# A gap of four words in the transposed tokens of the feed-forward: the first product reads a two-dimensional pattern

## The chip, the cores and the metric

The kernel runs on one core of a Trainium2 chip. The metric is the device time of one execution in microseconds; a profile of one execution gives its span, from the first to the last instruction.

## What is computed

Inputs are q, k, v of shape (8, 8, 576, 64) and two weights of a feed-forward, 512 x 2048 and 2048 x 512. Cut to what matters:

```python
out_d  = sm_attn(mean4(q), mean4(k), mean4(v))        # attention on tokens pooled by 4
out_up = repeat(out_d, 4)
scores = where(abs(i - j) < 4, q @ k.T / 8, -1e9)      # local attention
x = heads_to_channels(out_up + softmax(scores) @ v)    # (8, 576, 512)
mixed = real(fft(fft(x, axis=1), axis=2))
u  = x + mixed
un = (u - mean(u)) / sqrt(var(u) + 1e-6)               # over the 512 channels
result = u + maximum(un @ w_ch1, 0) @ w_ch2
```

## The kernel before

The 8 x 576 = 4608 tokens make 36 tiles of 128. The first third of the execution is attention and the mixing of tokens and channels. Then comes the feed-forward, which the change touches. It goes over nine blocks (class `Block`) of four tiles, 512 tokens, and in each block over f = 0 to 15, the sixteen slices of 128 hidden channels.

Before a block, each of its four tiles is normalised (`un`), transposed on TensorE in four pieces of 128 x 128 (`turn`, L733), and split into a high part (`turn_high`, ScalarE, L739, rounds to float32r) and the remainder (`turn_low`, VectorE, L742). Both parts are written into `unT`, of which there are two: `unT0` for the blocks 0, 2, 4, 6, 8 and `unT1` for the blocks 1, 3, 5, 7. In each partition `unT` holds, for the part x and the channel slice c, the 512 tokens of the block in a row; `turned` gives the place of one tile of 128 in it.

For each f, `first` (L762) makes twelve matmuls into one PSUM bank `hps`: for the four channel slices c, `w1h` with the high part, `w1l` with the high part, `w1h` with the low part. The weight slice of 128 x 128 is stationary, and the 512 tokens in `unT[:, x, c, :]` move. ScalarE takes the relu into `hh` (L766), VectorE the remainder into `hl` (L770), and `second` makes twelve matmuls (L780 to L782) into four accumulators `acc`, one for each tile, with `hh` or `hl` stationary and `w2h` or `w2l`, 512 words in a row, moving. So a block has 16 x 12 first and 16 x 12 second products. At its end VectorE adds `acc` to the tokens (L786), and they are stored.

The weights' high and low parts stay in SBUF for the whole feed-forward. Those of f = 0 and 1 lie in the pool `res`, those of f = 2 to 4 in the pool `pt`, 5 to 8 in `middle`, the others in `more`. `unT0` lies in the pool `early`, `unT1` in `middle`; these pools are opened at `close_b`, `close_a`, `close_e` and `close_d`, when the tiles of the earlier stages at their places are no longer used.

The order of all work is written out by hand: `at(t, fn)` puts each step into a list with a nominal time, and the steps are issued to their engines in the order of those times. In `Block.plan`, the second product of f comes after the first product of f + 1, and the transposes of the next block's tiles are put between the groups of the current block.

Two other places matter to the reading of the profile. In the channel mix, the last matmul of a group (L609) has the moving operand `signs.unsqueeze(1).to_broadcast([P, HD, 2])`: 256 times the same two words. The mask of the local attention (L388) moves 64 words of bfloat16 eight times over.

Of the kernel before, what the change touches and what calls it, by code (L numbers as in the profile page):

```python
# [9 lines left out]
F32R = mybir.dt.float32r  # L10
# [47 lines left out]
TILES = 4  # L58
# [7 lines left out]
def kernel(  # L66
# [14 lines left out]
    nc = tc.nc  # L81
    P = 128
# [4 lines left out]
    NCC = DM // P  # L87
# [23 lines left out]
    def weight_tiles(pool, fs, which=(1, 2)):  # L111

        for f in fs:
            for w in which:
                shape = [P, NCC, P] if w == 1 else [P, DM]
                wts[f, w] = [pool.tile(shape, F32R, name=f"w{w}{part}{f}", bufs=1) for part in "hl"]
# [11 lines left out]
    unTs = {}  # L128
# [85 lines left out]
    pools = {}  # L214

    def bank(name, rows=P):
        banks.append(banks.pop(0))
        return banks[-1].tile([P, DM], F32, name=name, tag="ps")[:rows]
# [135 lines left out]
    class Unit:  # L354
# [123 lines left out]
        def plan(self):  # L478
            t = 4 * self.u
            for fn, (first, step) in ((self.load, AT["qk"]), (self.sum_in, AT["sums"])):  # L480
                at(pooled_at(self.b) + first + step * self.m, fn)
            at(t + AT["load_v"][0], self.load_v)
            stages = [self.scores, self.maxima, self.exps, self.transpose_p, self.copy_p, self.values, self.result]
            for d, fn in zip(AT["local_steps"], stages):
                at(t + d, fn)
# [22 lines left out]
    class Mix:  # L508
# [130 lines left out]
        def plan(self):  # L639
            t = mix_at(self.b)  # L640

            local = list(reversed(range(NSL)))
            first, step, first_m, step_m = AT["halves"]
            for i, slot in enumerate(local):
                at(t + first + step * i, self.half_sum, slot)
                at(t + first_m + step_m * i, self.half_difference, slot)
            for begin, name, these in (
                (pooled_end(self.b), "pooled_splits", (NSL, NSL + 1)),
                (t, "splits", local),
            ):  # L650
                first, step, odd, high, low = AT[name]
                for i, slot in enumerate(these):
                    u = begin + first + step * i
                    at(u, self.channels_even, slot)
                    at(u + odd, self.channels_odd, slot)
                    at(u + high, self.split_high, slot)
                    at(u + low, self.split_low, slot)
# [25 lines left out]
    def pool(name, bufs=1, **kw):  # L683
        return ctx.enter_context(tc.tile_pool(name=name, bufs=bufs, reuse_waits="tile", **kw))
# [3 lines left out]
    class Block:  # L688
# [44 lines left out]
                nc.tensor.transpose(tp[:, c * P : (c + 1) * P], self.un[i][:, c * P : (c + 1) * P], ident)  # L733

        def turned(self, i, x):
            return unTs[self.n % 2][:, x, :, i * P : (i + 1) * P]

        def turn_high(self, i):
            nc.scalar.copy(out=self.turned(i, 0), in_=self.tp[i].rearrange("p (c n) -> p c n", c=NCC))  # L739
# [15 lines left out]
        def first(self, f):  # L755

            unT = unTs[self.n % 2]
            w1h, w1l = wts[f, 1]
            hps = self.hps[f] = bank("hps")[:, : TILES * P]
            mms = [(a, x, c) for a, x in ((w1h, 0), (w1l, 0), (w1h, 1)) for c in range(NCC)]  # L760
            for i, (a, x, c) in enumerate(mms):
                nc.tensor.matmul(hps, a[:, c, :], unT[:, x, c, :], start=(i == 0), stop=(i == len(mms) - 1))  # L762

        def high(self, f):
            hh = self.hh[f] = pools["pt"].tile([P, TILES * P], F32R, name="hh", bufs=2)
# [65 lines left out]
    def close_b():  # L831
        p1.close()
        pools["early"] = pool("early")
        unTs[0] = pools["early"].tile([P, 2, NCC, TILES * P], F32R, name="unT0")

    def close_a():
        plocal.close()
# [8 lines left out]
    def close_e():  # L846
        pseq.close()
        middle = pool("middle")
        unTs[1] = middle.tile([P, 2, NCC, TILES * P], F32R, name="unT1")
        weight_tiles(middle, range(*CHUNKS[1:3]))  # L850

    def close_d():
        pmix.close()
        weight_tiles(pool("more"), range(*CHUNKS[2:]))

    at(t_b, close_b)
    at(t_a, close_a)
    at(t_e, close_e)
    at(t_d, close_d)
    for i in range(TILES):  # L860
# [9 lines left out]
    t = t_a + AT["ffn"][0]  # L870
    starts = {}
    for n, f0, f1 in [(0, 0, ROUND), (1, 0, ROUND), (0, ROUND, NF)] + [(n, ROUND * (n == 1), NF) for n in range(1, NBLK)]:
        starts[n] = t
        t = blocks[n].plan(t, f0, f1)
# [15 lines left out]
    t = 0.0  # L890
    for n, x in enumerate(quarters):
        if x.f < CHUNKS[0]:
            decode(n, first + step * n, ahead)
        else:
            begin = [t_a + ahead_later, t_e, t_d][sum(x.f >= c for c in CHUNKS[1:3])]
            t = max(t + step_later, begin + 0.3)
# [139 lines left out]
```

## Time and profile before

| | |
|---|---|
| time, median of 3 runs | 1229.01 us |
| lowest and highest run | 1224.79 and 1229.82 us |
| span of the profiled execution | 1224.5 us (the page gives no time for it beside the span) |
| mean granted TensorE clock | 0.979 |
| PE busy | 1175.8 us, 8336 matmuls |
| first product, L762 | 1728 matmuls of 128 x 128 by 128 x 512 |
| second product, L780 to L782 | 1728 matmuls of the same shape |
| a whole block of the feed-forward | 89.46 to 89.50 us |

How to read it: PE is TensorE's matmul row, PEld its weight loads, which run beside matmuls. The recorded duration of a matmul reaches into the next one, so the price of a matmul in a dense stretch is the distance from its start to the next start. In a timeline a row may stand for several instructions (x4) that follow one another; the first number is the start of the first of them in microseconds from the span's start.

### The profile page before, as it was taken

Reading aid. Unit: us, or ns where it says so; the run is one execution under the profiler, and the core shown is the slowest. Engines: PE = TensorE matmul, PEld = TensorE weight load, DVE = VectorE, ACT = ScalarE, POOL = GpSimd, SP = SyncE. Lnnn points to the kernel's source line nnn. Section 1 sums busy time; section 2 is a strip of 40 time slices with the busy share of each in tenths; the row PEclk is TensorE's granted clock in tenths of the full one; section 3 lists DMA queues with packets and bytes.
Section 4 is the critical chain, followed back from the end, with each engine's and each line's share of the span. In section 5 each row is a group of like instructions: output and inputs, shape, how many; then the busy total and the mean of one; then the engine's idle time right before and its main releaser. Section 6 shows DMA issues by size and latency. Waiting matters only on the chain.

```text
span 1224.5 us, 20569 instructions
## 1 busy us (share of the span) xinstructions
PE 1175.8 (96%) x8336; PEld 977.2 (80%) x8336; DVE 596.9 (49%) x1218; ACT 356.1 (29%) x1038; POOL 321.0 (26%) x397
## 2 busy tenths in 40 slices
PE   5799999999997799999999999999999999999998
PEld 4687887888885677888888888888888888888887
DVE  3778887998969789834122222222221222221212
ACT  2655556655553334411011111011111111111110
POOL 2326356447528466620100100100100100100000
PEclk7899999999998899999999999999999999999999
DMA  9855565667624444440400400400400400300000
GB/s 289 224 169 163 171 180 163 189 196 207 167 69 138 118 134 120 130 112 1 103 2 1 103 1 1 104 1 1 104 1 1 103 1 1 103 1 1 35 1 35
DMA packets 50462, 111.45 MB, mean 91 GB/s; under 512 B 6120, under 2 KB 6248, under 8 KB 50040
## 3 DMA queue, kind: packets, MB, share of 16 engines
q1 hardware_dynamic: 42000, 88.66, 22.5%
q0 software_dynamic: 8368, 21.48, 9.6%
q8 instruction: 66, 1.08, 0.4%
q14 instruction: 28, 0.23, 0.1%
HBM read 81.82 MB, written 28.34 MB: 90 GB/s over the span
## 4 chain that ended last, share of the span: by engine, by line
PE 77%; DVE 11%; DMA 5%; issue 3%; POOL 2%; ACT 1%; SPq 0%; DVEq 0%; POOLq 0%; ACTq 0%
PE hps L762 31%; PE acc L780 10%; PE acc L782 10%; PE acc L781 10%; PE y L571 4%; PE mix L609 3%; PE av L454 2%; DMA vsum<-in_vg_dram 2%; PE avd L309 1%; DMA raw<-in_wq_dram 1%; PE sc L395 1%; DMA ud<-odt 1%; DVE sums L381 1%; PE tpn L733 1%; DVE wt L174 1%
## 5 line engine op out<-in xcount | busy, mean ns | idle before, releaser
L770 DVE SCALAR_TENSOR_TENSOR hl<-hps,hh 128x512 fp32r<-128x512 f32 x144 | 99.3, 690 | 460.1 <-ACT hh L766 460.1
L762 PE MATMUL hps<-unT,w1h 128*128 128x512 f32 x1152 | 311.5, 392 | 0.0
L762 PEld LDWEIGHTS hps<-unT,w1h 128*128 128x128 f32 x1152 | 216.3, 189 | 45.9 <-DVE unT L742 0.3
L766 ACT ACTIVATE hh<-hps 128x512 fp32r<-128x512 f32 x144 | 86.1, 598 | 515.8 <-PE hps L762 515.8
L780 PE MATMUL acc<-w2h,hh 128*128 128x512 f32 x576 | 227.5, 395 | 1.7 <-DVE ut L786 1.6
L782 PE MATMUL acc<-w2h,hl 128*128 128x512 f32 x576 | 225.6, 392 | 0.2 <-DVE hl L770 0.2
L781 PE MATMUL acc<-w2l,hh 128*128 128x512 f32 x576 | 225.0, 391 | 0.0
L762 PE MATMUL hps<-unT,w1l 128*128 128x512 f32 x576 | 155.7, 392 | 0.0
L780 PEld LDWEIGHTS acc<-w2h,hh 128*128 128x128 f32 x576 | 108.3, 188 | 25.6 <-DVE ut L786 1.5
L782 PEld LDWEIGHTS acc<-w2h,hl 128*128 128x128 f32 x576 | 108.3, 188 | 24.7 <-DVE hl L770 1.3
L762 PEld LDWEIGHTS hps<-unT,w1l 128*128 128x128 f32 x576 | 108.8, 189 | 23.6
L781 PEld LDWEIGHTS acc<-w2l,hh 128*128 128x128 f32 x576 | 108.3, 188 | 22.1
L718 POOL TENSOR_TENSOR rstd<-rstd,mhalf 128x1 f32<-128x1 f32 x36 | 20.5, 571 | 340.4 <-DVE rstd L717 340.4
L705 POOL DMA_DIRECT2D ut<-ud x40 | 36.2, 1154 | 207.8 <-DMA ut<-um 207.7
L413 ACT ACTIVATE sb<-sc,mx 128x64 f32<-128x64 f32 x320 | 69.8, 329 | 1.3
L609 PE MATMUL mix<-chanm,yh 128*128 128x512 f32 (+1 forms) x192 | 65.8, 425 | 3.1 <-DVE xs L613 2.0
L549 POOL TENSOR_TENSOR fl<-xeo,fh 128x512 fp32r<-128x512 f32 (+1 forms) x40 | 55.1, 1383 | 43.5 <-ACT fh L544 43.5
L454 PE MATMUL av<-vaug,pT 64*64 64x65 f32 x1280 | 48.4, 225 | 6.9 <-POOL pT L442 4.9
L454 PEld LDWEIGHTS av<-vaug,pT 64*64 64x64 f32 x1280 | 42.5, 138 | 15.6 <-POOL pT L442 5.1
L522 POOL TENSOR_TENSOR xm<-xa,xb 128x512 f32<-128x512 f32 x24 | 32.9, 1372 | 81.5 <-DVE xb L472 70.6
L742 DVE TENSOR_TENSOR unT<-tpn,unT 128x512 fp32r<-128x512 f32 x36 | 24.7, 687 | 55.2 <-ACT unT L739 55.2
L395 PEld LDWEIGHTS sc<-qkT 64*64 64x64 f32 x1280 | 46.5, 141 | 3.5 <-issue 0.8
(102 smaller groups left out, 1552.6 us busy)
## 6 DMA issues: line engine op xcount, KB each, us to landing
qkT<-in_qk_dram SPq DMA_DIRECT2D x40, 512.0 KB
raw<-in_wq_dram SPq DMA_DIRECT2D x64, 256.0 KB
vaug<-in_vw_dram SPq DMA_DIRECT2D x40, 260.0 KB
ud<-odt SPq DMA_DIRECT2D x16, 576.0 KB
out_dram<-ut SPq DMA_DIRECT2D x36, 256.0 KB
ut<-um SPq DMA_DIRECT2D x32, 256.0 KB
ut<-ud POOLq DMA_DIRECT2D x32, 256.0 KB, 5.4
vsum<-in_vg_dram POOLq DMA_DIRECT2D x24, 292.5 KB, 4.8
```

Source lines behind the costliest of these rows:

```text
L395: nc.tensor.matmul(sc[r, a * W : (a + 1) * W], self.qkT[r, 0, a // 2, o : o + W], self.qkT[r, 1, a // 2, o : o + W], start=False, stop=Tru ...
L413: nc.scalar.activation(out=self.sb[:, a], in_=self.sc[:, a * W : (a + 1) * W], func=AF.Exp, scale=0.125, bias=self.mx[:, a : a + 1],)
L454: nc.tensor.matmul(av[r, a, :], pT[r, 4 * hh + a], va[r, 4 * hh + a, :], start=True, stop=True)
L549: nc.gpsimd.tensor_sub(out=l, in0=self.x[t], in1=h.bitcast(F32))
L571: nc.tensor.matmul(y, l, r, start=(i == 0), stop=(i == len(mms) - 1))
L609: nc.tensor.matmul(to, l, r, start=(i == 0), stop=(i == len(mms) - 1))
L762: nc.tensor.matmul(hps, a[:, c, :], unT[:, x, c, :], start=(i == 0), stop=(i == len(mms) - 1))
L766: nc.scalar.activation(out=hh, in_=self.hps[f], func=AF.Relu)
L770: nc.vector.scalar_tensor_tensor(out=hl, in0=self.hps[f], scalar=0.0, in1=self.hh[f].bitcast(F32), op0=ALU.max, op1=ALU.subtract)
L780: nc.tensor.matmul(acc, hh, w2h, start=start, stop=False)
L781: nc.tensor.matmul(acc, hh, w2l, start=False, stop=False)
L782: nc.tensor.matmul(acc, hl, w2h, start=False, stop=stop)
```

## The change

Both `unT` get a gap of four words (16 bytes) after each run of tokens: `unT0` has four runs of 128 tokens, 132 words apart, `unT1` has two runs of 256 tokens, 260 words apart. `turned` finds a tile's place in the new layout, and `first` reads the runs as a pattern of two dimensions and names its output in PSUM, which lies as before, by the same two dimensions. `unT0` takes 512 bytes more in each partition, `unT1` 256.

```diff
         def turned(self, i, x):
-            return unTs[self.n % 2][:, x, :, i * P : (i + 1) * P]
+            u = unTs[self.n % 2]
+            n = TILES // u.shape[3]
+            return u[:, x, :, i // n, i % n * P : i % n * P + P]
...
             hps = self.hps[f] = bank("hps")[:, : TILES * P]
+            n = unT.shape[3]
             mms = [(a, x, c) for a, x in ((w1h, 0), (w1l, 0), (w1h, 1)) for c in range(NCC)]
             for i, (a, x, c) in enumerate(mms):
-                nc.tensor.matmul(hps, a[:, c, :], unT[:, x, c, :], start=(i == 0), stop=(i == len(mms) - 1))
+                nc.tensor.matmul(
+                    hps.rearrange("p (n t) -> p n t", n=n),
+                    a[:, c, :],
+                    unT[:, x, c, :, : TILES * P // n],
+                    start=(i == 0),
+                    stop=(i == len(mms) - 1),
+                )
...
-        unTs[0] = pools["early"].tile([P, 2, NCC, TILES * P], F32R, name="unT0")
+        unTs[0] = pools["early"].tile([P, 2, NCC, TILES, P + 4], F32R, name="unT0")
...
-        unTs[1] = middle.tile([P, 2, NCC, TILES * P], F32R, name="unT1")
+        unTs[1] = middle.tile([P, 2, NCC, 2, TILES // 2 * P + 4], F32R, name="unT1")
```

## The prediction

> **What bounds the kernel now.** I read the head of the page first: the engines' busy time, the span in 40 slices and the chain that ended last.
>
> ```profile
> span 1224.5 us, 20569 instructions
> PE 1175.8 (96%) x8336; PEld 977.2 (80%) x8336; DVE 596.9 (49%) x1218; ACT 356.1 (29%) x1038; POOL 321.0 (26%) x397
> PE   5799999999997799999999999999999999999998
> PEclk7899999999998899999999999999999999999999
> PE 77%; DVE 11%; DMA 5%; issue 3%; POOL 2%; ACT 1%; SPq 0%; DVEq 0%; POOLq 0%; ACTq 0%
> PE hps L762 31%; PE acc L780 10%; PE acc L782 10%; PE acc L781 10%; PE y L571 4%; PE mix L609 3%; PE av L454 2%; DMA vsum<-in_vg_dram 2%; PE avd L309 1%; DMA raw<-in_wq_dram 1%; PE sc L395 1%; DMA ud<-odt 1%; DVE sums L381 1%; PE tpn L733 1
> ```
>
> TensorE is busy 96% of the span, the granted clock is full in the last two thirds, and the chain runs 77% through PE. The first product of the feed-forward (L762), the line that the change edits, is 31% of the chain. So what one of its 1728 matmuls gains or loses is seen in the end. The windows on whole blocks of four token tiles confirm it:
>
> ```profile
> 593.46:682.92 89.46, 89.46 (x401) 73.70 (x400) 21.79 (x40) 11.62 (x20) 6.61 (x9) 1.00 0.14 36
> 1040.80:1130.30 89.50, 89.50 (x402) 73.74 (x401) 21.79 (x40) 11.62 (x20) 5.73 (x8) 1.00 0.14 36
> ```
>
> The columns are length, then busy time of PE, PEld, DVE, ACT and POOL, the granted clock, the DMA share and GB/s. PE has no gap in a block; DVE (21.8 of 89.5) and ACT (11.6) have much room.
>
> The recorded duration of a matmul (390 ns) overlaps with the next, so its price is the distance from one start to the next. The timeline gives it: a settled group in the middle of a block, the start of a block, and a group after the transposes of the next block's tokens.
>
> ```profile
> 638.41 1.07 PE L762 MATMUL hps<-unT,w1h 128*128 128x512 f32 x4
> 639.32 1.07 PE L762 MATMUL hps<-unT,w1l 128*128 128x512 f32 x4
> 640.23 1.07 PE L762 MATMUL hps<-unT,w1h 128*128 128x512 f32 x4
> 641.13 0.39 PE L780 MATMUL acc<-w2h,hh 128*128 128x512 f32 x1
> ...
> 643.86 0.39 PE L762 MATMUL hps<-unT,w1h 128*128 128x512 f32 x1
> ```
>
> ```profile
> 593.46 1.10 PE L762 MATMUL hps<-unT,w1h 128*128 128x512 f32 x4
> 594.39 1.09 PE L762 MATMUL hps<-unT,w1l 128*128 128x512 f32 x4
> 595.33 1.10 PE L762 MATMUL hps<-unT,w1h 128*128 128x512 f32 x4
> 596.26 0.40 PE L780 MATMUL acc<-w2h,hh 128*128 128x512 f32 x1
> ```
>
> ```profile
> 618.39 0.60 PE L733 MATMUL tpn<-ident,un 128*128 128x128 f32 x4
> 618.74 0.48 PE L780 MATMUL acc<-w2h,hh 128*128 128x512 f32 x1
> 619.05 0.40 PE L781 MATMUL acc<-w2l,hh 128*128 128x512 f32 x1
> ...
> 621.60 0.39 PE L762 MATMUL hps<-unT,w1h 128*128 128x512 f32 x1
> ```
>
> Settled, twelve first products take 641.13 - 638.41 = 2.72 us, 227 ns each, and twelve second products 643.86 - 641.13 = 2.73 us, the same. At the block's start, where the weights are those of f = 0, in a pool of their own, twelve take 596.26 - 593.46 = 2.80 us, 233 ns each. After the transposes eleven take 621.60 - 619.05 = 2.55 us, 232 ns each, and then the pace settles. So the pace of the same instruction depends on where its operands lie and on what ran just before; it is not a fixed price.
>
> **What a two-dimensional read costs here.** The trace has two matmuls of 512 columns whose moving operand is a two-dimensional pattern: the signs in the channel mix (256 runs of two words, f32r) and the mask (8 runs of 64, bf16). Their rows in the views by tile, with those of the first product:
>
> ```profile
> L609 PE MATMUL mix<-signs,yz x24: 377/378/380, 90.1 to 436.2; 128*128 128x512 f32 x16, 128*64 128x512 f32 x8
> L388 PE MATMUL sc<-maskb,identb x80: 375/376/632, 15.6 to 354.9; 64*64 64x512 bf16 x80
> L762 PE MATMUL hps<-unT,w1h x1152: 387/390/775, 389.6 to 1214.8; 128*128 128x512 f32 x192
> L762 PE MATMUL hps<-unT,w1l x576: 386/390/629, 390.5 to 1213.9; 128*128 128x512 f32 x192
> L739 ACT CAST unT<-tpn x36: 578/587/589, 378.8 to 1111.4; 128x512 fp32r<-128x512 f32 x36
> L742 DVE TENSOR_TENSOR unT<-tpn,unT x36: 675/691/693, 381.4 to 1112.0; 128x512 fp32r<-128x512 f32 x36
> ```
>
> The slowest of the 24 sign matmuls (380) is shorter than the fastest of 1728 first products (386); the medians differ by 12 ns. The starts say the same in a place where a sign matmul stands between one-dimensional ones of the same shape:
>
> ```profile
> 426.74 0.40 PE L609 MATMUL mix<-chanm,yh 128*128 128x512 f32 x1
> 426.98 0.40 PE L609 MATMUL mix<-chanm,yl 128*128 128x512 f32 x1
> 427.21 0.38 PE L609 MATMUL mix<-signs,yz 128*128 128x512 f32 x1
> 427.42 0.40 PE L780 MATMUL acc<-w2h,hh 128*128 128x512 f32 x1
> 427.66 0.40 PE L781 MATMUL acc<-w2l,hh 128*128 128x512 f32 x1
> ```
>
> Distances: 0.24, 0.23, then 0.21 for the sign matmul, then 0.24 again. So wrapping from run to run costs nothing there, 256 times over, and the contiguous read of 512 words is the slower one. What the rows do not separate: both two-dimensional patterns read few words again and again (step 0), while the changed unT reads 512 different ones. That is the point on which the forecast stands or falls.
>
> [...]
>
> **The change, part by part.**
> - The first product, 1728 matmuls (9 blocks x 16 f x 12): same count, same weights, same 512 columns. unT0 (blocks 0, 2, 4, 6, 8) is read as 4 runs of 128, unT1 (the four odd blocks) as 2 runs of 256. Ends of the price: 12 ns less (the sign row) and 6 ns more (233 against 227, the pace at which the same read goes in its unsettled form). I take the sign row, as the nearest with this kind of pattern, for both tiles: 1728 x 12 = 20.7 us less, all on the path, since PE has no gap.
> - The second product (L780 to L782) is not edited, but it follows a group with another pace, and the rows after the transposes show that a disturbed pace needs about eleven matmuls to settle: 11 x (232 - 227) = 55 ns for a group. If it happens in each of the 144 groups: 8 us back; if in none: 0. I take 25 ns for a group, under half, because the transposes are a harsher break than a change of pace: 3.6 us back.
> - The writers of unT (L739 on ACT, L742 on DVE, 36 each): they already write four runs of 128, at steps of 512 words; the step becomes 528 or 520. Instruction count and elements stay. I cost it at nothing: both engines are mostly idle in a block, and their 587 and 691 ns lie beside PE's second products. If that cover were gone, 36 x 0.1 us, for a tenth of a microsecond more each, would be 4 us.
> - The output view of hps: still 512 contiguous words; nothing.
> - Memory: unT0 grows by 512 bytes in each partition, unT1 by 256, so tiles above them move up by as much. That may change which freed tile a new one waits for between 370 and 590 us, where pools change over. No row prices it: 0 taken, 3 us either way kept for the range.
> - No wait, DMA or queue entry is added, and none moved past another.
>
> Sum: -20.7 + 3.6 = -17.1 us. The profiled execution has a span of 1224.5 us, so its span would become 1207.4. The median of the three runs, 1229.0, is 4.5 above that span; taking the same difference off the median gives 1212.
>
> **Rivals.**
> 1. No change: 1229. The sign and mask matmuls are fast because they read the same few words again, not because they are two-dimensional, and a run of 128 different words is read at the pace of 512. For it: the mask is bf16, the signs are two words. Against it: the pace of the contiguous read does vary with placement, so it isn't at a limit of bandwidth. [...]
> 2. Slower by a lost lock. The settled pace needs the moving read and the weight load beside it to fall into step; the gap shifts every run by four words against the weights, the step is lost, and every first product goes at 233. Place: groups now settled, about 144 less the 18 of f = 0 and 1 in nine blocks; price 0.08 us each (2.80 - 2.72), 126 x 0.08 = 10 us, 1239; with the second product disturbed after each, 126 x 0.055 = 7 us more, 1246. It shows as slower once more than half of those groups (6 of 10 us) are unsettled. For it: the f = 0 groups, where only the weights' place differs. Against it: the settled pace comes back by itself after each break.
> 3. Slower by a restart. The 12 ns that a contiguous read has over the sign matmul is a price for beginning a read, and each run pays it: unT0 3 x 12 x 960 matmuls = 35 us, unT1 1 x 12 x 768 = 9 us, 1273. Against it: 256 runs of the sign matmul pay nothing. It decides from 2 ns a run on (about 7 us).
>
> **How the numbers follow.** A measurement of this kernel tells some 0.5% (6 us) from no change: its three runs lie 5 us apart. Forecast: 0.46, own range 1204 (no second product disturbed: 1208; the 18 groups of f = 0 and 1 lose their 0.08 us too: 1 us; the memory's 3 us fall on the good side) to 1222 (every second product disturbed, 1216, and a third of the 12 ns not won, 7 us). No change 0.26. Lost lock 0.19, restart 0.09. So faster 0.46, same 0.26, slower 0.28. The range 1204 to 1242 leaves out the restart and the worst of the lost lock above, and a little below: some 2 in 10.
>
> **What would show it.** Right: the median duration of L762 in the view by tile near 378, twelve first products in about 2.58 us, blocks of 89.5 us near 87.5, even and odd blocks alike. Rival 1: 390 and 89.5 as before. Rival 2: L762 at 396 with groups of 2.80 us, blocks above 90. Rival 3: even blocks some 7 us longer, odd ones 2. Even and odd blocks that differ would say that the length of a run counts. Wrong in its second step: L780 to L782 with starts of 0.23 to 0.24 throughout after faster first products. The forecast fails if the sign matmul's pace comes from its few words.

## The result, and the profile after

The change made the kernel slower: 1233.51 us (median of 10 runs, 1229.19 to 1236.84) against 1226.05 (1221.06 to 1230.08), ratio 1.006 with a 95% interval of 1.004 to 1.0079. That is 0.6%: small, but clear of the noise. The profiled execution took 1230.93 us, with a span of 1229.2. The head of its page and the line of the chain:

```profile
span 1229.2 us, 20578 instructions
PE 1179.9 (96%) x8336; PEld 974.2 (79%) x8336; DVE 597.2 (49%) x1218; ACT 356.4 (29%) x1038; POOL 318.5 (26%) x397
...
PE hps L765 31%; PE acc L789 10%; PE acc L790 10%; PE acc L791 10%; PE y L571 4%; PE mix L609 4%; PE av L454 2%; DMA vsum<-in_vg_dram 2%; PE sc L395 2%; PE avd L309 2%; DMA raw<-in_wq_dram 1%; DMA ud<-odt 1%; DVE sums L381 1%; PE tpn L733 1
```

The same 8336 matmuls keep PE busy 4.1 us longer. The busy times of the others moved by 3 us at most (PEld 977.2 to 974.2, POOL 321.0 to 318.5, DVE and ACT 0.3 each), and none of them bounds a block. The windows on one even block (unT0, four runs) and one odd block (unT1, two runs) show where:

```profile
592.13:682.18 90.05, 90.05 (x401) 73.67 (x400) 21.79 (x40) 11.62 (x20) 6.62 (x9) 1.00 0.14 36
682.18:772.77 90.59, 90.59 (x402) 73.62 (x400) 21.77 (x40) 11.63 (x20) 5.73 (x8) 1.00 0.14 35
```

Both were 89.47 before. If all nine blocks lose as much, five even blocks by 0.58 and four odd ones by 1.12 make 7.4 us, about the difference of the medians (7.5). In the two profiled executions themselves the stretch from the third block to the end grew by 6.0 us, from 631.0 (1224.5 - 593.46) to 637.1 (1229.2 - 592.13); the stretch before it came out 1.3 us shorter, so the spans differ by 4.7 only. PE still has no gap: the matmuls follow one another more slowly. The view by tile has it in the durations of the first product (medians 390 before), and the timeline in its starts, for an even and an odd block:

```profile
L765 PE MATMUL hps<-unT,w1h x1152: 388/393/774, 386.7 to 1219.4; 128*128 128x512 f32 x192
L765 PE MATMUL hps<-unT,w1l x576: 388/393/618, 387.6 to 1218.5; 128*128 128x512 f32 x192
```

```profile
648.66 1.08 PE L765 MATMUL hps<-unT,w1h 128*128 128x512 f32 x4
...
651.43 0.39 PE L789 MATMUL acc<-w2h,hh 128*128 128x512 f32 x1
...
654.17 0.40 PE L765 MATMUL hps<-unT,w1h 128*128 128x512 f32 x1
...
710.49 1.09 PE L765 MATMUL hps<-unT,w1h 128*128 128x512 f32 x4
...
713.28 0.39 PE L789 MATMUL acc<-w2h,hh 128*128 128x512 f32 x1
...
716.02 0.39 PE L765 MATMUL hps<-unT,w1h 128*128 128x512 f32 x1
```

Twelve first products take 2.77 us in the even block and 2.79 in the odd one (2.72 when settled before), and the twelve second products after them 2.74 (2.73). Start by start, the twelve of the even block repeat with the four channel slices: 234, 230, 225, 234 ns, then twice 231, 230, 225, 234. The slices lie 64 bytes further on each, modulo 256, so the pace seems to go with the place of what is read. The groups no longer settle at 227 ns, and the two dimensions bring nothing: no matmul is near the sign matmul's 378 ns.

### The profile page after: what moved, and what is told of

The parts are those of the page before. It is cut to its first block, busy times and chain, and to the rows that moved or that the text cites. A ratio compares the mean times of both kernels' runs of the same rounds, so it can differ in the third digit from the quotient of the medians.

```text
span 1229.2 us, 20578 instructions
## 1 busy us (share of the span) xinstructions
PE 1179.9 (96%) x8336; PEld 974.2 (79%) x8336; DVE 597.2 (49%) x1218; ACT 356.4 (29%) x1038; POOL 318.5 (26%) x397
## 4 chain that ended last, share of the span: by engine, by line
PE 79%; DVE 11%; DMA 5%; issue 2%; POOL 2%; ACT 1%; SPq 1%; DVEq 0%; POOLq 0%; ACTq 0%
PE hps L765 31%; PE acc L789 10%; PE acc L790 10%; PE acc L791 10%; PE y L571 4%; PE mix L609 4%; PE av L454 2%; DMA vsum<-in_vg_dram 2%; PE sc L395 2%; PE avd L309 2%; DMA raw<-in_wq_dram 1%; DMA ud<-odt 1%; DVE sums L381 1%; PE tpn L733 1%; PE sp L264 1%
## 5 line engine op out<-in xcount | busy, mean ns | idle before, releaser
L549 POOL TENSOR_TENSOR fl<-xeo,fh 128x512 fp32r<-128x512 f32 (+1 forms) x40 | 52.5, 1318 | 46.8 <-ACT fh L544 46.8
L741 ACT CAST unT<-tpn 128x512 fp32r<-128x512 f32 x36 | 21.1, 586 | 97.6 <-PE tpn L733 97.6
```

Source lines behind the costliest of these rows:

```text
L549: nc.gpsimd.tensor_sub(out=l, in0=self.x[t], in1=h.bitcast(F32))
```

## The experiments

Each kernel was profiled in one execution. What is compared is the length of blocks, from the starts of three successive blocks in the timeline (an even block, then an odd one); this length repeats within 0.05 us inside one execution. Of the kernels in this section only the last was timed more than once. Numbers of bytes below that the kernels' shapes and paddings don't give are places of tiles in the compiled programs, which no trace holds.

**Runs without a gap.** Does a pattern of several dimensions cost or bring anything?

```diff
         def turned(self, i, x):
+            i = (0, 2, 1, 3)[i]
             return unTs[self.n % 2][:, x, :, i * P : (i + 1) * P]
...
-                nc.tensor.matmul(hps, a[:, c, :], unT[:, x, c, :], start=(i == 0), stop=(i == len(mms) - 1))
+                m = unT[:, x, c, :].rearrange("p (h t n) -> p t h n", h=2, t=2)
+                to = hps.rearrange("p (t h n) -> p t h n", h=2, t=2)
+                nc.tensor.matmul(to, a[:, c, :], m, start=(i == 0), stop=(i == len(mms) - 1))
```

> Before with the first product reading four runs of 128 words without any gap: tiles 1 and 2 of a block change places in unT, and the runs are read in the order 0, 2, 1, 3, so that the pattern cannot be merged into one of 512 words. All runs start where they did, at the same place within 64 bytes as the weights. Theory P (place: what counts is how the moving words lie against the weights within some 64 bytes, the number of runs is free): blocks of four tiles stay at 89.47 us, twelve settled first products take 2.72 us. Theory R (each further run costs): blocks of at least 90.05 us, as the even blocks of the changed kernel. A gain, blocks near 87, would mean that several dimensions help after all and that the gap spoils it.

```profile
591.32 1.10 PE L765 MATMUL hps<-unT,w1h 128*128 128x512 f32 x4
...
680.79 1.10 PE L765 MATMUL hps<-unT,w1h 128*128 128x512 f32 x4
...
770.26 1.10 PE L765 MATMUL hps<-unT,w1h 128*128 128x512 f32 x4
```

Both blocks take 89.47 us, to the hundredth what they took in one dimension. Here the dimensions cost nothing and bring nothing, and theory R falls. What is left is where the words lie.

**Gaps of 64 bytes.** The changed kernel with `P + 16` and `TILES // 2 * P + 16` in place of `+ 4`.

> The changed kernel with gaps of 16 words (64 bytes) in place of 4: the same runs, four of 128 in unT0 and two of 256 in unT1, but every run keeps its place within 64 bytes. Theory P: all blocks back at 89.47 us, settled groups of 2.72 us. Theory R: blocks as in the changed kernel, 90.05 to 90.09 even and 90.59 odd.

```profile
590.73 1.09 PE L765 MATMUL hps<-unT,w1h 128*128 128x512 f32 x4
...
682.02 1.09 PE L765 MATMUL hps<-unT,w1h 128*128 128x512 f32 x4
...
772.35 1.09 PE L765 MATMUL hps<-unT,w1h 128*128 128x512 f32 x4
```

A miss for theory P as it stood: 91.29 and 90.33 us. The even block is worse than with gaps of 16 bytes. So places 64 bytes apart are not alike; if the cost repeats with the place at all, its period is not 64 bytes.

**unT moved as a whole, one dimension.** First by 16 and 48 bytes, then by 32 bytes (even) and with a gap after each channel slice (odd):

```diff
-        unTs[0] = pools["early"].tile([P, 2, NCC, TILES * P], F32R, name="unT0")
+        flat = pools["early"].tile([P, 2 * NCC * TILES * P + 16], F32R, name="unT0")
+        unTs[0] = flat[:, 4 : 4 + 2 * NCC * TILES * P].rearrange("p (x c n) -> p x c n", x=2, c=NCC)
...
```

> Before, unT read as 512 words in a row, but moved as a whole: unT0 by 16 bytes, unT1 by 48. No gap and no second dimension. Theory P: the blocks slow down without either: even blocks (16 bytes) and odd blocks (48 bytes) between 89.9 and 91 us, settled groups between 2.73 and 2.81 us, not 2.72. Theory R: 89.47 us in both, as before.

```profile
593.56 1.09 PE L762 MATMUL hps<-unT,w1h 128*128 128x512 f32 x4
...
684.20 1.09 PE L762 MATMUL hps<-unT,w1h 128*128 128x512 f32 x4
...
775.17 1.09 PE L762 MATMUL hps<-unT,w1h 128*128 128x512 f32 x4
```

> Before, 512 words in a row: unT0 moved by 32 bytes, and in unT1 a gap of four words after each channel slice only, so that slice c lies 16 c bytes further. Theory P: even blocks: the groups of f = 0 and 1, which took 2.80 us, settle to 2.72, and those of the other f go from 2.72 to 2.80: blocks of 89.47 + 14 x 0.08 - 2 x 0.08 = 90.4 us or, with the second products disturbed too, up to 91; odd blocks slower than 89.47, with a pace that goes with c. Theory R: 89.47 us in both.

```profile
596.28 1.09 PE L762 MATMUL hps<-unT,w1h 128*128 128x512 f32 x4
...
687.32 1.08 PE L762 MATMUL hps<-unT,w1h 128*128 128x512 f32 x4
...
778.14 1.09 PE L762 MATMUL hps<-unT,w1h 128*128 128x512 f32 x4
```

90.64 and 90.97, then 91.04 and 90.82 us: kernels with neither a gap within a read nor a second dimension slow down more than the changed one. The two kernels don't isolate the named distances, since the padding also moved the later tiles by 64 or 128 bytes against one another. That gave a further hint: where w2 came to lie 128 bytes off hh (f from 5 on in the second of them), the second products were slow too, 2.77 to 2.80 us for twelve (the last matmul of an even block is recorded with 0.40 us there, and with 0.39 before), while in the changed kernel, where the padding moved them by 256 bytes, they nearly settle (2.74). And the group of f = 0 did not settle in the even blocks of the second kernel, where unT and its weights agree modulo 64 bytes: its first four are recorded with 1.09 us, against 1.07 when settled. The shortest period that fits all of it is 256 bytes; the last three experiments test it.

**Few words, read again.** Why is the sign matmul fast?

```diff
-                nc.tensor.matmul(hps, a[:, c, :], unT[:, x, c, :], start=(i == 0), stop=(i == len(mms) - 1))
+                if self.n % 2:
+                    m = unT[:, x, c, :P].unsqueeze(1).to_broadcast([P, TILES, P])
+                else:
+                    m = unT[:, x, c, :2].unsqueeze(1).to_broadcast([P, 2 * P, 2])
...
```

> Before, but the first product does not read its tokens: in even blocks its moving operand is 256 times the same two words of unT, in odd blocks four times the same 128 words. Everything else is as before; the tokens' other words are left out of the product. Theory Q (meeting: the moving read and the load of the next weights walk through SBUF at the same time and hinder each other where they meet modulo some 256 bytes; a read of few words does not walk): even blocks at the sign matmul's pace, 216 ns, so 89.47 - 192 x 0.012 = 87.2 us; odd blocks as before, 89.47, since four times 512 bytes is the same walk modulo 256. Theory S (words that were read just before come cheap): odd blocks gain as well, up to three quarters of the even ones' gain. Theory D, on which the prediction was built (several dimensions are fast in themselves), has been contradicted by e1_runs_no_gap; it would give 87.2 in both.

```profile
589.38 1.03 PE L767 MATMUL hps<-unT,w1h 128*128 128x512 f32 x4
...
649.60 1.02 PE L767 MATMUL hps<-unT,w1h 128*128 128x512 f32 x4
...
652.19 0.39 PE L785 MATMUL acc<-w2h,hh 128*128 128x512 f32 x1
...
654.96 0.38 PE L767 MATMUL hps<-unT,w1h 128*128 128x512 f32 x1
...
676.80 1.10 PE L767 MATMUL hps<-unT,w1h 128*128 128x512 f32 x4
...
766.23 1.02 PE L767 MATMUL hps<-unT,w1h 128*128 128x512 f32 x4
```

With the same two words the blocks take 87.42 us, and twelve first products 652.19 - 649.60 = 2.59 us, 216 ns each: the sign matmul's pace (215 to 217 ns from start to start in the trace of before, where the next matmul follows at once), with the same weights loaded. The second products after them don't settle: 654.96 - 652.19 = 2.77 us. Four times the same 128 words take 89.43 us, as 512 different ones do. So a read that stays on two words is enough to give the sign matmul's pace, and 128 words read four times are not "few".

**The other side, the weight load.** Three kernels change how the weights of the next matmul are read: every second word of interleaved slices, one word 128 times, and interleaved for both products.

```diff
-                shape = [P, NCC, P] if w == 1 else [P, DM]
+                shape = [P, NCC // 2, P, 2] if w == 1 else [P, DM]
...
-                nc.tensor.matmul(hps, a[:, c, :], unT[:, x, c, :], start=(i == 0), stop=(i == len(mms) - 1))
+                nc.tensor.matmul(hps, a[:, c // 2, :, c % 2], unT[:, x, c, :], start=(i == 0), stop=(i == len(mms) - 1))
```

> Before with w1 stored word by word from two channel slices in turn, so that the load of a weight slice takes every second word and walks 8 bytes a weight instead of 4. The trace before has 108 ns for 128 weights (the transposes' pace) and 213 to 216 ns for 512 moving words, so the moving read walks twice as fast as the load and overtakes it; now both walk equally fast and keep their distance. Same result. Theory Q: settled first products at 216 ns, twelve in 2.59 us, blocks near 89.47 - 192 x 0.011 = 87.4; a distance of zero that does not open by itself could instead make it slower. Rival (an inherent 11 ns of a contiguous read, or a strided load that is slow in itself): 89.47 or more.

```profile
593.48 1.08 PE L769 MATMUL hps<-unT,w1h 128*128 128x512 f32 x4
...
683.83 1.08 PE L769 MATMUL hps<-unT,w1h 128*128 128x512 f32 x4
...
774.19 1.08 PE L769 MATMUL hps<-unT,w1h 128*128 128x512 f32 x4
```

In the next, `a[:, c, :1].to_broadcast([P, P])` is stationary:

> Before, but the first product's stationary operand is one word 128 times, so that the weight load stays at one place; the other weights are left out. Moving operand as before. Theory Q: the pace changes, to 216 ns if a load of the same word needs no further read (blocks 87.4). Rival (the 11 ns above the sign matmul belong to the moving read alone): settled groups stay at 2.72 us, blocks near 89.47.

```profile
593.79 1.09 PE L762 MATMUL hps<-unT,w1h 128*128 128x512 f32 x4
...
683.83 1.09 PE L762 MATMUL hps<-unT,w1h 128*128 128x512 f32 x4
...
773.81 1.09 PE L762 MATMUL hps<-unT,w1h 128*128 128x512 f32 x4
```

> As e6_w1_interleaved, and the stationary operands of the second product too: hh and hl are written word by word from two token tiles in turn, so their loads also walk 8 bytes a weight; VectorE's part for hl is two instructions in place of one. Same result. Theory Q: settled second products at 216 ns as well, blocks near 89.47 - 384 x 0.011 = 85.2 us, time near 1221 - 9 x 4.2 = 1183. Rival: 89.47 or more, or more still if the strided writes of ScalarE and VectorE come late for PE (hh 0.6 us and hl 0.7 us before).

```profile
596.92 1.10 PE L769 MATMUL hps<-unT,w1h 128*128 128x512 f32 x4
...
688.56 1.10 PE L769 MATMUL hps<-unT,w1h 128*128 128x512 f32 x4
...
780.20 1.10 PE L769 MATMUL hps<-unT,w1h 128*128 128x512 f32 x4
```

None brought the hoped gain: the even blocks take 90.35, 90.04 and 91.64 us. The recorded weight loads, before and in the first two of these kernels:

```profile
L762 PEld LDWEIGHTS hps<-unT,w1h x1152: 186/188/333, 389.4 to 1214.6; 128*128 128x128 f32 x192
...
L769 PEld LDWEIGHTS hps<-unT,w1h x1152: 192/193/200, 394.3 to 1220.9; 128*128 128x128 f32 x192
...
L762 PEld LDWEIGHTS hps<-unT,w1h x1152: 185/188/332, 389.9 to 1218.7; 128*128 128x128 f32 x192
```

The interleaved load is recorded as 5 ns longer (193 against 188), so the rival named before, a strided load that is slow in itself, stays possible for the two interleaved kernels. The load of one word lasts 188 ns as before; in its blocks nothing but the weights' read changed, and the pace of the matmuls changed all the same, as theory Q had it, but to the slower side (90.04 us for an even block against 89.47). So the two reads do act on each other. The simple picture of two reads that go through the memory at different speeds, of which one overtakes the other, found no support: neither equal steps nor a load that stays in one place brought the pace of 216 ns. Its speeds were the author's estimate, from the 107 to 110 ns between the starts of the transposes and the 215 to 217 ns of the sign matmul; that the first of these is the time of a weight load is not shown: beside the first products the loads are recorded with 188 ns, beside the transposes with 140.

**The period, with a gap sixteen times as long.** One gap in the middle of each 512 words, 256 bytes in unT0 and 128 in unT1, slices 2304 bytes apart; `step` is the number of words from one run of 256 to the next:

```diff
+            step = 288 if self.n % 2 else 320
...
+                m = bass.AP(tensor=m.tensor, offset=m.offset, ap=[m.ap[0], [step, 2], [1, 256]])
```

> Two runs of 256 words in every unT, with one gap between them: 64 words (256 bytes) in unT0, 32 words (128 bytes) in unT1. The channel slices are 2304 bytes apart, nine times 256, and no other tile moves against another modulo 256. Theory P256 (place against the weights modulo 256 bytes; e1 to e4 leave 256 as the smallest period that fits): even blocks 89.47 us, settled groups of 2.72 us, although the gap is sixteen times that of the change; odd blocks slower, between 90 and 91.5. If the period is 128 bytes, both stay at 89.47; if a gap costs in itself, both are slower.

```profile
593.93 1.10 PE L766 MATMUL hps<-unT,w1h 128*128 128x512 f32 x4
...
683.40 1.08 PE L766 MATMUL hps<-unT,w1h 128*128 128x512 f32 x4
...
773.74 1.10 PE L766 MATMUL hps<-unT,w1h 128*128 128x512 f32 x4
```

89.47 and 90.34 us: a gap of 256 bytes costs nothing, one of 128 bytes does. This is the changed kernel's form, two runs and a gap, with and without its cost.

**64 and 16 words.** As with the few words above, `unT[:, x, c, :64]` eight times and `[..., :16]` 32 times.

> As e5_same_words, with 8 times the same 64 words (256 bytes) in even blocks and 32 times the same 16 words (64 bytes) in odd ones; the other tokens' words are left out of the product. Theory P256: 8 times 256 bytes is the same walk modulo 256 as 512 words in a row, so even blocks as before, 89.43 to 89.47 us; in odd blocks the read stays within a quarter of the places, so the pace changes: less meeting with the load, 87.4 to 89 us. Rival (only a read that stays within one place is fast): odd blocks not faster than 89.4.

```profile
597.66 1.10 PE L766 MATMUL hps<-unT,w1h 128*128 128x512 f32 x4
...
687.12 1.14 PE L766 MATMUL hps<-unT,w1h 128*128 128x512 f32 x4
...
704.23 1.12 PE L766 MATMUL hps<-unT,w1h 128*128 128x512 f32 x4
...
707.13 0.40 PE L784 MATMUL acc<-w2h,hh 128*128 128x512 f32 x1
...
779.59 1.10 PE L766 MATMUL hps<-unT,w1h 128*128 128x512 f32 x4
```

Eight times 256 bytes take 89.46 us, as 2048 bytes in a row, as a period of 256 bytes has it. The second half missed: a read within 64 bytes is not faster but the slowest of all, 92.47 us, with 707.13 - 704.23 = 2.90 us for twelve. Of the reads tried here only the one of two words is faster than 227 ns on the mean of a group.

**The first weights in place.** If the place modulo 256 bytes against the loaded weights is what counts, the unsettled groups of f = 0 and 1 can be cured by moving their weights: they lay at 128, all other weights, unT, hh and hl at 32.

```diff
     wts = {}
+    res.tile([P, 40], F32, name="pad0")
     weight_tiles(res, range(CHUNKS[0]))
+    res.tile([P, 24], F32, name="pad1")
```

> Before, with a tile of 160 bytes ahead of the weights of f = 0 and 1 and one of 96 bytes behind them, so that these weights lie at the same place modulo 256 bytes as unT, hh and hl, as the other weights do already. Same result. Theory P256: the groups of f = 0 and 1 settle too. First products of f = 0 to 3 from 2.81, 2.81, 2.76, 2.76 us to 2.72; second products of f = 0 and 1 from 2.80 and 2.81 to 2.72: blocks from 89.47 to 89.02 us, in sum 4 us or 0.3% faster. Rival (the first groups of a block are slow for another reason, such as the loads and stores of tokens at that time): 89.47, no change.

```profile
597.23 1.07 PE L764 MATMUL hps<-unT,w1h 128*128 128x512 f32 x4
...
599.95 0.39 PE L782 MATMUL acc<-w2h,hh 128*128 128x512 f32 x1
...
686.25 1.07 PE L764 MATMUL hps<-unT,w1h 128*128 128x512 f32 x4
...
775.28 1.07 PE L764 MATMUL hps<-unT,w1h 128*128 128x512 f32 x4
```

Blocks of 89.02 and 89.03 us, the forecast to the hundredth; the first group of a block takes 599.95 - 597.23 = 2.72 us where it took 2.80. Its time is 1222.18 us (median of 12 runs) against 1225.85 (median of 17), ratio 0.9979, interval 0.9958 to 1.0001. The gain of 0.45 us in each block is plain in the profile; in the whole time a gain of that size (4 us, 0.3%) lies inside the interval, which just includes 1. By the length of its blocks it is the fastest version here that computes the whole result; that its whole time is shorter than before is not shown.

## Why the prediction was wrong

It forecast 1212 us, and the kernel went to the other side. That 1233.5 lies inside the range, which reached to 1242, is no success: a part of rival 2 had been taken into the range, and the mechanism that was forecast brought nothing.

The step that failed is the price of the first product: "I take the sign row, as the nearest with this kind of pattern, for both tiles: 1728 x 12 = 20.7 us less". The text had named the flaw itself, that both two-dimensional rows read few words again and again. The run without a gap and the run on two words show what holds in its place: 0 from the dimensions, all 11 ns from staying on two words. Rival 1's reason was right for the signs, though its outcome, no change, was not; the mask's 64 words of bfloat16 were not tested by themselves, and 64 words of float32r, eight times over, brought nothing. The forecast chose its row by one likeness, the number of dimensions, and passed over what the trace showed to change the price: the groups of f = 0 and 1 ran at 233 ns with one and the same pattern, and only their weights lay elsewhere.

The sum built on this price was sound under its own condition. With two words in place of 512 the block takes 87.42 us, near the 87.5 that the text names as the sign of being right. The change did not fulfil that condition.

Rival 2, the lost lock, is what came; it had a chance of 0.19. It was right on the place (every settled group, even and odd blocks) and on the kind (the moving words shifted against the weights); its price was too high. It assumed 2.80 us for each group, the pace of f = 0; measured are 2.77 (even) and 2.79 (odd). It added 0.055 us for each second product; measured is 0.01 to 0.02 in the two groups above, since these settle after about five matmuls in place of eleven. So 10 to 17 us became 7.4. Blocks "above 90" is what the profile shows; 90.05 and 90.59 differ with the places at which the two layouts put the runs: at 32 + 64 c + 16 t modulo 256 in unT0, at 32 + 32 c + 16 r in unT1 (first part of the tokens, slice c, run t or r), where the weights lie at 32 for f from 2 on. Which of these places costs how much is not worked out.

Rival 3, a price for each run, is refuted by the runs without a gap (0.00 us for three further runs).

The costs set to nothing held: ACT and DVE write unT in 587 and 691 ns as before, the output in PSUM lies as before, and the third block starts at 592.13 us against 593.46, so the moved tiles cost nothing that is seen. The second product's step, 3.6 us in the sum, had the right sign and about the size (0.01 to 0.02 us x 144 is 1.4 to 2.9). That is partly luck, as it was meant for first products that become faster. Where they did, in the blocks on two words, the group shown lost 0.04 us (2.77 against 2.73), where 0.025 was forecast.

Set side by side, the blocks of 512 words in one run (89.47 us) are matched by four runs without a gap (89.47) and by two runs with a gap of 256 bytes (89.47), and not by gaps of 128 bytes (90.34), 64 (91.29 and 90.33) and 16 (90.05 and 90.59). And where the weights lie counts by itself: with the moving words as before, the weights of f = 0 and 1 moved by 160 bytes took the first group of a block from 2.80 to 2.72 us.

What stays open: why a settled group goes at 227 ns and not at 216 when more than two words are read; how the two reads act on each other; and why a disturbed group needs several matmuls to settle (five in the changed kernel, about eleven after the transposes).

## What to carry to other kernels

Before taking a price from a row of another operand, ask in which respects the rows differ, and test the one that the trace shows to matter; here it was placement, seen in two groups of the same instruction at 2.80 and 2.72 us. In dense float32r matmuls like these, try the moving operand and the weights loaded beside it at the same place modulo 256 bytes: other placements of the same 512 words made a block 0.6 to 2.0% longer (90.05 to 91.29 us against 89.47), and a gap of 256 bytes between runs was free.

## What the runs showed of the hardware that was not expected

- The pace of a 512-column float32r matmul depends on where its moving words lie against the weights that are loaded meanwhile, as far as these runs show by the distance modulo 256 bytes: 227 ns at distance 0 in a settled group (2.72 us for twelve), with a gap of 256 bytes or none alike (89.47 us for a block), and more at every other placement tried: on the mean of a group 231 and 233 ns (2.77 and 2.79 us for twelve) in the changed kernel, and blocks of 90.33 to 91.29 us with the other gaps and shifts.
- It is 216 ns when the moving read is the same two words (2.59 us for twelve), the same as with 512 different words for 64 or 128 read again (blocks of 89.46 and 89.43 us against 89.47), and about 242 ns for 16 (2.90 us for twelve).
- Four runs without a gap cost nothing against one run of 512 words (89.47 us for a block in both).
